# Logits of two batches as row sums on VectorE instead of transposes and matmuls on TensorE

## Chip, core and metric

One core of a Trainium2 chip runs the whole program. The metric is the time of one execution in microseconds (us) as the device counts it. Of the kernel before there are three timed runs and one profiled run.

## What is computed

Three layers follow one another: a causal attention with a decay, an up and down projection with a squared ReLU, and a layer of eight experts in which every expert takes 288 of the 2304 tokens, chosen by the size of their gate logits. In the change only the logits matter:

```python
x = attention(q, k, v, f)            # 2304 tokens of 512, in 4 batches of 576
h = np.maximum(x @ w_in, 0.0)        # 512 -> 2048
x2 = h * h @ w_out                   # 2048 -> 512
logits = x2 @ w_gate                 # 512 -> 8, float32
order = np.argsort(-logits.flatten())
# tokens are given to experts in this order, 288 to each
out[mask] = np.maximum(x2[mask] @ w1[e], 0.0) @ w2[e]     # for every expert e
```

## The kernel before

Every operation is entered as a task with the engines that may do it, an estimated cost on each, the buffers it reads and writes and a priority (`s.base`, then the order of entry; a lower number goes first). `Sched.run` (line 169) plays the whole program through once with these costs, gives each free engine the ready task of the lowest number, and so fixes for each engine the order of its instructions. On the chip each engine works in that order and waits for what is not ready.

The middle layer works in chunks of 256 tokens, `moe1_chunk(b, c)` (line 725), for batch b and half c, in the order (0,1), (0,0), (1,1), (1,0), (2,1), (2,0), (3,1). A chunk has 16 steps f. In a step `moe1_up` (line 683) makes 128 of the 2048 columns: 12 matmuls of 256 columns (lines 691 to 693: high by high, low by high, high by low part), then ScalarE takes the ReLU (696) and the square (697), a rounded high part `hh` is made, and the rest `hl` = r - `hh` (line 708) on GpSimd or VectorE. Two steps later `moe1_down` (lines 715 to 717) adds this step's six matmuls of 512 columns to two accumulators `acc`, one for each 128 tokens.

At the end of a chunk `x2_tail` (line 802) runs once for each of the two accumulators: the accumulator is copied to SBUF (`x2_rows`, line 791), stored to `x2d` in HBM, transposed by TensorE in four blocks (line 809), copied to SBUF again (812), multiplied with the gate matrix `wg` (line 817: four matmuls with 8 columns, each in two passes), and copied into the table of logits `L` (819). The buffers for rows and transposed rows are the two raw-weight buffers `wraw`; the transposes and logits use the two PSUM buffers `u` of the up projection.

The last two chunks, (3,0) and the 64 first tokens of all batches, go through `moe1_last` (line 744). It gets its logits in another way: `gate_weights` (line 822) sums on VectorE the products of each row of `w_out` and each gate column (16 blocks x 8 experts, line 835), so that the logits follow from the squared hidden values by short matmuls (lines 757, 758). The gate's columns for that lie on all partitions in `wgb`, loaded by one DMA from `wgT`. These tasks have priority 12, the chunks 3 + 2b.

The pools of these late stages open at barriers in the plan: `pp` and `gp` when the attention's tasks are done, `hp` (the hidden values of `moe1_last`) when the tasks of `gp` are done.

The routing (`phase`, line 934) takes the logits of the first three batches as one part and the rest as another, and sets the gather of the first expert's rows (line 1167) and with it the experts' matmuls (lines 1254 to 1288).

Of the kernel before, what the change touches and what calls it, by code (L numbers as in the profile page):

```python
# [8 lines left out]
F = mybir.dt.float32  # L9
R = mybir.dt.float32r  # L10
BF = mybir.dt.bfloat16
# [3 lines left out]
OP = mybir.AluOpType  # L15
# [4 lines left out]
B, H, S, D = 4, 8, 576, 64  # L20
NT, DM, DFF, E, FE = 2304, 512, 2048, 8, 1024
# [15 lines left out]
P0 = None  # L37
HV = [0]
NSM = 4
ABASE = (0, 0.5, 0.6, 2)  # L40
HM = 50.0
LM = 40.0
# [278 lines left out]
def dve1(n):  # L321
    return 70 + 1.04 * n
# [6 lines left out]
def act(n, psum=False, extra=0):  # L329
    return (51 if psum else 93) + 0.833 * n + 93 * extra  # L330
# [19 lines left out]
LO_ENG = ["pool"]  # L350
# [3 lines left out]
def hi_alts(n, engs="act pool"):  # L354
    a = {}
    for e in engs.split():
        a[e] = {"act": act(n), "pool": pts(n), "dve": dve2(n)}[e]
    return a


def lo_alts(n, engs=None):
    a = {}
    engs = engs or LO_ENG[0]
    for e in engs.split():
        a[e] = {"pool": ptt(n), "dve": dve1(n)}[e]
    return a


class K:
# [355 lines left out]
    def moe1_chunk(self, b, c):  # L725
        s = self.s
        xh, xl = self.moe1_x(b, c)
        acc = [s.buf(self.ps, [128, 512], F, "acc", 2) for _ in range(2)]

        def down(f):  # L730
            for t in range(2):
                self.moe1_down(f, t, acc[t], *prev[f])
        prev = []
        for f in range(16):
            prev.append(self.moe1_up(f, xh, xl))
            if f >= 2:
                down(f - 2)
        down(14)
        down(15)
        for t in range(2):  # L740
            self.x2_tail(b, c, t, acc[t])


    def moe1_last(self, chunks):
# [40 lines left out]
                self.x2_rows(b, c, t, acc[t])  # L785
        self.x2_done = s.tasks[-3]

    def x2_rows(self, b, c, t, acc):
        s, mp = self.s, self.mp
        xr = s.buf(mp, [128, 512], F, "x2r", 0, also=[("wraw", 0), ("wraw", 1)])  # L790
        s.op({"act": act(512, True), "dve": dve1(512)}, lambda e: self.rnd(e, xr.t, acc.t), r=[acc], w=[xr])
        tt = (b * 4 + c * 2 if b < B else 16) + t
        if b < B:
            tok = b * S + 64 + c * 256 + t * 128
            self.dma(lambda: self.x2d[tok:tok + 128, :], lambda: xr.t, 128 * 2048, r=[xr], w=[(self.x2d, tt)])
        else:
            for j in range(2):
                tok = (2 * t + j) * S
                self.dma(lambda tok=tok: self.x2d[tok:tok + 64, :], lambda j=j: xr[64 * j:64 * j + 64], 64 * 2048, r=[xr], w=[(self.x2d, (tt, j))])
        return xr, tt  # L800
# [18 lines left out]
        s.op({"act": act(8, True), "dve": dve1(8)}, lambda e: self.rnd(e, self.L[:, tt, :], pl[:, :E]), r=[pl], w=[(self.L, tt)])  # L819


    def gate_weights(self):
        s = self.s
        gp = self.gp
        wb = s.buf(gp, [128, E, DM], F, "wgb")
        self.dma(lambda: wb.t.rearrange("p e d -> p (e d)"), lambda: self.wgT.t.rearrange("e d -> (e d)")[None, :].to_broadcast([128, DM * E]), 128 * 16384, r=[self.wgT], w=[wb])
        Gf = s.buf(gp, [128, 16, E], F, "gf")
        G2 = self.G2 = s.buf(self.pp, [128, 16, 2 * E], R, "g2")
        for f in range(16):
            wo = s.buf(gp, [128, DM], F, "wof", 2)  # L830
            wh, wl = self.wu[self.unit(1, f, 0)]
            s.op(lo_alts(DM, "dve"), lambda e, f=f, wo=wo, wh=wh, wl=wl: e.tensor_add(wo.t, wh[:, f % 2].bitcast(F), wl[:, f % 2].bitcast(F)), r=[(wh, f % 2), (wl, f % 2)], w=[wo])
            for x in range(E):
                jk = s.buf(gp, [128, DM], BF, "gjk", 1)
                s.op({"dve": dve1(DM) + 85}, lambda e, f=f, x=x, wo=wo, jk=jk: e.tensor_tensor_reduce(  # L835
                    out=jk.t, in0=wo.t, in1=wb[:, x, :], scale=1.0, scalar=0.0, op0=OP.mult, op1=OP.add,
                    accum_out=Gf[:, f, x:x + 1]), r=[wo, wb], w=[jk, (Gf, (f, x))])
        n = 16 * E
        s.op(hi_alts(n, "act"), lambda e: self.rnd(e, G2[:, :, 0:E], Gf.t), r=[Gf], w=[G2])
        s.op({"dve": dve1(n)}, lambda e: e.tensor_sub(G2[:, :, E:], Gf.t, G2[:, :, 0:E].bitcast(F)), r=[Gf], w=[G2])  # L840
# [72 lines left out]
    def route_iotas(self):  # L913
# [4 lines left out]
        def bank():  # L918
            if not rt:
                rt.append(self.ps.tile([128, 512], F, name="ov0", tag="ov0", bufs=1))  # L920
            return rt[0]
        s.views["rt", 0] = lambda: bank()[:, 0:128]
        for j in range(NSM):
            s.views["rt", 1 + j] = lambda j=j: bank()[:, 128 + 64 * j:192 + 64 * j]
# [9 lines left out]
    def phase(self, m):  # L934
# [11 lines left out]
        def small(tag="sm"):  # L946

            if m == 0 and tag in ("H", "pl"):
                return s.buf(self.ps, [128, 512], F, tag + "0", 0, also=[("pt", 0)] if tag == "H" else [("sc", 0), ("sc", 1)])
            return s.buf(self.ps, None, F, tag, 0, also=[("rt", 0)] if tag == "H" else [("rt", 1 + j) for j in range(NSM)])  # L950

# [361 lines left out]
@with_exitstack  # L1313
def tile_kernel(ctx, tc, qT, kT, vP, f, w_in, w_out, w_gate, w1, w2, out, upto=9, dbg=None):
    k = K(ctx, tc, qT, kT, vP, f, w_in, w_out, w_gate, w1, w2, out)
    nc = tc.nc
    LO_ENG[0] = "pool"
    k.scat = []
    k.main_es, k.att_es = ExitStack(), ExitStack()
    s = k.s  # L1320
    k.early_pools()
    k.moe1_weights()
    k.att_pools()
    s.base = 0
    k.consts()
    k.cum()
    s.base = 50
    k.route_consts()
    s.base = 0
    s.base = 0  # L1330
    for b in range(B):
        s.base = ABASE[b]
        k.attention(b)
    s.base = 1
    s.pools["wraw"] = k.mp
    for which, r, c in [(w, r, c) for i in range(4) for w, r, c in [(0, r, i) for r in range(4)] + [(1, 4 * i + r, 0) for r in range(4)]]:
        t = k.unit(which, r, c)
        raws, was = [z for z in RS if z[1] > 2 * t + 1], [z for z in WS if z[1] > 2 * t + 1]
        hold = k.mark[0, WHD] if 4 * t > NE else None
        for half in [None] if raws else [0, 1]:  # L1340
            k.w_piece(which, r, c, half, raws or [("wraw", j) for j in range(2)], was, hold)
    s.base = 2
    k.gate_rows()
    for b in range(B):
        if b == 1:
            LO_ENG[0] = "dve pool"
        s.base = 3 + 2 * b
        for c in (1, 0) if b + 1 < B else (1,):
            k.moe1_chunk(b, c)

    def open_pp():
        k.att_es.close()
        k.pp.p = k.pool("pp", reuse_waits="tile")
        k.gp.p = k.pool("gp", ctx=k.gp_es, reuse_waits="tile")

    def open_hp():
        k.gp_es.close()
        k.hp.p = k.pool("hp", ctx=k.hp_es, reuse_waits="tile")

    def open_ep():  # L1360
        k.hp_es.close()
        k.main_es.close()
        k.ep.p = k.pool("ep", reuse_waits="tile")

    k.pp, k.gp, k.hp, k.ep = Late(), Late(), Late(), Late()
    k.gp_es, k.hp_es = ExitStack(), ExitStack()
    k.pp.bar = k.gp.bar = s.barrier(s.tasks_on(k.ao), open_pp)
    s.base = 12
    k.gate_weights()
    k.hp.bar = s.barrier(s.tasks_on(k.gp), open_hp)  # L1370
    s.base = 11
    k.moe1_last([(B - 1, 0), (B, 0)])
    k.ep.bar = s.barrier(s.tasks_on(k.xp, k.mp, k.hp), open_ep)
    LO_ENG[0] = "dve pool"
    s.base = 15
    k.route_iotas()
    for m in range(E):
        s.base = 20 + m
        idx, widx = k.phase(m)
        s.base = 30 + m  # L1380
        k.expert(m, idx, widx)
    order = s.run()
    s.emit(order)
# [34 lines left out]
```

## Time and profile before

| | us |
|---|---|
| median of three timed runs | 1013.84 |
| lowest and highest | 1009.37 and 1014.49 |
| profiled execution | 1011.21 |
| its span, first to last instruction | 1009.4 |

The profile is of one execution. A matmul that is listed as 0.28 us long overlaps with the next one, so what a piece of TensorE work takes out of the stream is read from the distance between starts. Idle time of an engine that nothing waits for costs nothing. PEclk is the granted TensorE clock: 1.00 is 2.4 GHz and 0.50 is 1.2 GHz.

### The profile page before, as it was taken

Reading aid. Unit: us, or ns where it says so; the run is one execution under the profiler, and the core shown is the slowest. Engines: PE = TensorE matmul, PEld = TensorE weight load, DVE = VectorE, ACT = ScalarE, POOL = GpSimd, SP = SyncE. Lnnn points to the kernel's source line nnn. Section 1 sums busy time; section 2 is a strip of 40 time slices with the busy share of each in tenths; the row PEclk is TensorE's granted clock in tenths of the full one; section 3 lists DMA queues with packets and bytes.
Section 4 is the critical chain, followed back from the end, with each engine's and each line's share of the span. In section 5 each row is a group of like instructions: output and inputs, shape, how many; then the busy total and the mean of one; then the engine's idle time right before and its main releaser. Section 6 shows DMA issues by size and latency. Waiting matters only on the chain. (4 is left out here: it accounts for less than half of the span.)

```text
span 1009.4 us, 17558 instructions
## 1 busy us (share of the span) xinstructions
PE 942.6 (93%) x6231; PEld 761.1 (75%) x6231; DVE 600.1 (59%) x1941; ACT 393.8 (39%) x1072; POOL 321.3 (32%) x439
## 2 busy tenths in 40 slices
PE   6897899899999999999999999995999989999996
PEld 3454555667789888989898899874777767778996
DVE  6899898974439999822223222476667786422231
ACT  4575676565534444434343356300101120224320
POOL 2555555652333333300010100001112041556921
PEclk9898899999999999999999999997899998999998
DMA  6668676542230101010100000015745541334410
GB/s 215 218 207 274 209 244 220 177 146 85 82 130 1 43 1 42 2 43 1 42 1 22 1 22 1 1 43 149 250 173 192 190 152 43 103 114 150 131 48 24
DMA packets 48616, 105.67 MB, mean 105 GB/s; under 512 B 10280, under 2 KB 18632, under 8 KB 48400
## 3 DMA queue, kind: packets, MB, share of 16 engines
q1 hardware_dynamic: 45456, 95.11, 28.5%
q0 software_dynamic: 3072, 9.44, 3.2%
q8 instruction: 49, 0.80, 0.3%
q14 instruction: 39, 0.32, 0.1%
HBM read 90.20 MB, written 14.33 MB: 104 GB/s over the span
## 5 line engine op out<-in xcount | busy, mean ns | idle before, releaser
L691 PE MATMUL u<-xh,z 128*128 128x256 f32 x512 | 148.9, 291 | 2.3 <-ACT r L696 1.9
L692 PE MATMUL u<-xh,z 128*128 128x256 f32 x512 | 145.6, 284 | 0.0
L693 PE MATMUL u<-xl,z 128*128 128x256 f32 x512 | 145.4, 284 | 0.0
L696 ACT ACTIVATE r<-u 128x256 f32<-128x256 f32 x144 | 54.7, 380 | 175.8 <-PE u L693 167.3
L835 DVE CUSTOM_DVE_ANT_0 gjk<-wof,wgb 128x512 bf16<-128x512 f32 x128 | 106.7, 833 | 11.6 <-ACT r L696 7.9
L691 PEld LDWEIGHTS u<-xh,z 128*128 128x128 f32 x512 | 98.1, 192 | 15.4 <-issue 3.1
L692 PEld LDWEIGHTS u<-xh,z 128*128 128x128 f32 x512 | 98.3, 192 | 8.1
L693 PEld LDWEIGHTS u<-xl,z 128*128 128x128 f32 x512 | 98.2, 192 | 0.0
L1283 PE MATMUL acc<-ehh,z 128*128 128x288 f32 x320 | 92.1, 421 | 0.0
L717 PE MATMUL acc<-z,hl 128*128 128x512 f32 x224 | 89.2, 398 | 1.9 <-POOL hl L708 1.6
L715 PE MATMUL acc<-z,hh 128*128 128x512 f32 x224 | 90.9, 406 | 0.0
L716 PE MATMUL acc<-z,hh 128*128 128x512 f32 x224 | 89.7, 400 | 0.0
L1254 PE MATMUL u<-exh,z 128*128 128x288 f32 x304 | 86.5, 420 | 0.1
L708 POOL TENSOR_TENSOR hl<-r,hh 128x256 fp32r<-128x256 f32 x64 | 56.0, 877 | 93.7 <-ACT hh L383 71.7
L708 DVE TENSOR_TENSOR hl<-r,hh 128x256 fp32r<-128x256 f32 x48 | 21.5, 447 | 92.9 <-ACT hh L383 79.9
L1206 POOL TENSOR_TENSOR z<-wr,z 128x512 fp32r<-128x512 f32 x48 | 61.1, 1305 | 48.0 <-ACT z L383 47.9
L523 ACT ACTIVATE p<-p,st 128x448 f32<-128x448 f32 (+4 forms) x109 | 59.9, 550 | 38.0 <-DVE st L516 36.2
L1283 PEld LDWEIGHTS acc<-ehh,z 128*128 128x128 f32 x320 | 57.5, 194 | 15.9 <-issue 1.6
L511 POOL TENSOR_TENSOR row<-maskb,row 128x128 f32<-128x128 bf16 (+1 forms) x90 | 46.5, 523 | 67.4 <-DVE st L516 39.3
L1254 PEld LDWEIGHTS u<-exh,z 128*128 128x128 f32 x304 | 55.5, 194 | 14.6 <-DVE exh L387 0.3
L697 ACT ACTIVATE r<-r 128x256 f32<-128x256 f32 x138 | 57.6, 418 | 4.1
L1167 POOL DMA_INDIRECT xg<-x2d,ph_idx x24 | 25.6, 1069 | 98.6 <-DVE ph_P L1109 51.9
(350 smaller groups left out, 2175.8 us busy)
## 6 DMA issues: line engine op xcount, KB each, us to landing
z<-in_w_dram SPq DMA_DIRECT2D x36, 512.0 KB
wr<-in_w_dram SPq DMA_DIRECT2D x24, 512.0 KB
z<-in_w_in_dram SPq DMA_DIRECT2D x16, 512.0 KB
z<-in_w_out_dram SPq DMA_DIRECT2D x14, 512.0 KB
row<-cumd SPq DMA_DIRECT2D x24, 288.0 KB
xd<-xo SPq DMA_DIRECT2D x16, 288.0 KB
wraw<-rd SPq DMA_DIRECT2D x32, 128.0 KB
xa<-xd SPq DMA_DIRECT2D x8, 512.0 KB
```

Source lines behind the costliest of these rows:

```text
L523: s.op({"act": act(w, extra=2)}, lambda e, x=x, si=si, i=i, n=n, w=w, p=p[x], st=st[x]: e.activation(p[:n, :w], p[:n, :w], AF.Exp, bias=st ...
L691: e.matmul(u[:, :256], wh[:, k % 2, fs], xh[k][1](), start=(k == 0), stop=False)
L692: e.matmul(u[:, :256], wl[:, k % 2, fs], xh[k][1](), start=False, stop=False)
L693: e.matmul(u[:, :256], wh[:, k % 2, fs], xl[k][1](), start=False, stop=(k == 3))
L708: s.op(lo_alts(256), lambda e: e.tensor_sub(hl(), r.t, hh().bitcast(F)), r=[r, kh], w=[kl])
L715: g = [lambda e: e.matmul(acc.t, hh()[:, ts], wh[:, f % 2], start=(f == 0), stop=False), lambda e: e.matmul(acc.t, hh()[:, ts], wl[:, f % ...
L716: lambda e: e.matmul(acc.t, hh()[:, ts], wl[:, f % 2], start=False, stop=False),
L717: lambda e: e.matmul(acc.t, hl()[:, ts], wh[:, f % 2], start=False, stop=(f == 15))]
L835: s.op({"dve": dve1(DM) + 85}, lambda e, f=f, x=x, wo=wo, jk=jk: e.tensor_tensor_reduce(out=jk.t, in0=wo.t, in1=wb[:, x, :], scale=1.0, sc ...
L1206: s.op(lo_alts(512, LOE(m, which, i, 0, c)), lambda e, cs=cs: e.tensor_sub(lo[:, cs], raw[:, cs], hi[:, cs].bitcast(F)), r=[(raw, key), (h ...
L1254: s.op({"pe": 1.69 * CAP}, lambda e, k=k: e.matmul(u[:, :CAP], whi[0][k][:, fs], xh[k].t, start=(k == 0), stop=(k == 3)), r=[(whi[0][k], c ...
L1283: e.matmul(acc[:, :CAP], wh[:, ds], hh.t, start=(f == 0), stop=(f == 7))
```

## The change

The chunks of batches 1 and 2 (four chunks, eight accumulators) call a new function `x2_sums` instead of `x2_tail`. It copies the accumulator to a buffer `x2g` that takes the place of one of the attention's two `xo` buffers, stores it to `x2d` as before, and then issues eight VectorE instructions. Each multiplies the 128 x 512 rows with one gate column that lies on all partitions and adds along the row into one column of `L`. The transposes, the copy of the transposed rows, the logit matmuls and the copy of the logits of these chunks are gone. Each sum has a planned cost of 887 ns on VectorE.

For that the load of `wgb` is taken out of `gate_weights` into `gate_load`, and it and the barrier that opens `pp` and `gp` are entered ahead of the chunks. The load has priority 2 instead of 12. The barrier of `hp` now also waits in the plan for the eight times eight sums, since they use `gp`.

```diff
+DL = (1, 2)
...
         for t in range(2):
-            self.x2_tail(b, c, t, acc[t])
+            (self.x2_sums if b in DL else self.x2_tail)(b, c, t, acc[t])
...
+    def x2_sums(self, b, c, t, acc):
+        s = self.s
+        xr = s.buf(self.xp, [128, DM], F, "x2g", 0, also=[("xo", 0), ("xo", 1)])
+        xr.after = self.gp.bar
+        xr, tt = self.x2_rows(b, c, t, acc, xr)
+        for x in range(E):
+            jk = s.buf(self.gp, [128, DM], BF, "gjs", 1)
+            s.op({"dve": dve1(DM) + 285}, lambda e, x=x, jk=jk: e.tensor_tensor_reduce(
+                out=jk.t, in0=xr.t, in1=self.wgb[:, x, :], scale=1.0, scalar=0.0, op0=OP.mult, op1=OP.add,
+                accum_out=self.L[:, tt, x:x + 1]), r=[xr, self.wgb], w=[jk, (self.L, tt)])
...
-    def x2_rows(self, b, c, t, acc):
+    def x2_rows(self, b, c, t, acc, xr=None):
         s, mp = self.s, self.mp
-        xr = s.buf(mp, [128, 512], F, "x2r", 0, also=[("wraw", 0), ("wraw", 1)])
+        xr = xr or s.buf(mp, [128, 512], F, "x2r", 0, also=[("wraw", 0), ("wraw", 1)])
...
+    def gate_load(self):
+        s = self.s
+        wb = self.wgb = s.buf(self.gp, [128, E, DM], F, "wgb")
+        self.dma(lambda: wb.t.rearrange("p e d -> p (e d)"), lambda: self.wgT.t.rearrange("e d -> (e d)")[None, :].to_broadcast([128, DM * E]), 128 * 16384, r=[self.wgT], w=[wb])
+
     def gate_weights(self):
         s = self.s
         gp = self.gp
-        wb = s.buf(gp, [128, E, DM], F, "wgb")
-        self.dma(lambda: wb.t.rearrange("p e d -> p (e d)"), lambda: self.wgT.t.rearrange("e d -> (e d)")[None, :].to_broadcast([128, DM * E]), 128 * 16384, r=[self.wgT], w=[wb])
+        wb = self.wgb
...
     k.gate_rows()
+    k.pp, k.gp, k.hp, k.ep = Late(), Late(), Late(), Late()
+    k.gp_es, k.hp_es = ExitStack(), ExitStack()
+    k.pp.bar = k.gp.bar = s.barrier(s.tasks_on(k.ao), open_pp)
+    k.gate_load()
     for b in range(B):
...
             k.moe1_chunk(b, c)
...
-    k.pp, k.gp, k.hp, k.ep = Late(), Late(), Late(), Late()
-    k.gp_es, k.hp_es = ExitStack(), ExitStack()
-    k.pp.bar = k.gp.bar = s.barrier(s.tasks_on(k.ao), open_pp)
     s.base = 12
     k.gate_weights()
```

## Rows read from the trace of the kernel before

**Rows 1.** The profile's page, part 1: busy time, share of the span, instructions of each engine.

```profile
PE 942.6 (93%) x6231; PEld 761.1 (75%) x6231; DVE 600.1 (59%) x1941; ACT 393.8 (39%) x1072; POOL 321.3 (32%) x439
```

**Rows 2.** Busy time by stage: two chunks of the middle stretch; the columns stand first.

```profile
core 0: us, PE busy (x) PEld busy (x) DVE busy (x) ACT busy (x) POOL busy (x), PEclk, DMA share, GB/s
...
340.00:390.00 50.00, 48.96 (x315) 43.74 (x314) 48.06 (x113) 22.29 (x55) 17.77 (x19) 1.00 0.07 22
...
440.00:490.00 50.00, 49.96 (x326) 45.29 (x326) 10.51 (x23) 19.50 (x49) 4.18 (x7) 1.00 0.08 22
```

**Rows 3.** TensorE in order of time, end of chunk (1,1): start, length, work, count, wait.

```profile
384.50 0.60 PE L809 MATMUL u<-ident,wraw 128*128 128x128 f32 x4
385.36 0.66 PE L809 MATMUL u<-ident,wraw 128*128 128x128 f32 x4 [0.26 <-ACT r L696]
385.78 0.48 PE L715 MATMUL acc<-z,hh 128*128 128x512 f32 x1
...
387.24 1.84 PE L817 MATMUL u<-wg,wraw 128*128 128x8 f32 x16
388.94 0.37 PE L691 MATMUL u<-xh,z 128*128 128x256 f32 x1
```

**Rows 4.** The same view, end of chunk (1,0).

```profile
433.07 1.29 PE L809 MATMUL u<-ident,wraw 128*128 128x128 f32 x8
434.12 0.48 PE L715 MATMUL acc<-z,hh 128*128 128x512 f32 x1
...
435.09 1.85 PE L817 MATMUL u<-wg,wraw 128*128 128x8 f32 x16
436.79 0.41 PE L691 MATMUL u<-xh,z 128*128 128x256 f32 x1
```

**Rows 5.** The same view, end of chunk (2,0).

```profile
531.30 1.09 PE L809 MATMUL u<-ident,wraw 128*128 128x128 f32 x8
532.32 0.50 PE L715 MATMUL acc<-z,hh 128*128 128x512 f32 x1
...
534.02 1.95 PE L817 MATMUL u<-wg,wraw 128*128 128x8 f32 x16 [0.38 <-DVE wraw L387]
535.83 0.45 PE L691 MATMUL u<-xh,z 128*128 128x256 f32 x1
```

**Rows 6.** Busy time, columns as in Rows 2, behind the second and the fourth chunk end.

```profile
436.98:440.25 3.27, 3.27 (x14) 2.98 (x14) 0.16 (x1) 0.00 (x0) 0.00 (x0) 0.50 0.00 0
...
536.00:539.30 3.30, 3.30 (x14) 3.01 (x14) 3.22 (x17) 0.00 (x0) 0.00 (x0) 0.50 0.00 0
```

**Rows 7.** VectorE's existing row sums, line 835: ns min/median/max, starts; then the page's mean.

```profile
L835 DVE CUSTOM_DVE_ANT_0 gjk<-wof,wgb x128: 676/693/1257, 300.3 to 422.3; 128x512 bf16<-128x512 f32 x128
L835 DVE DVE_READ_ACCUMULATOR2_ANT gf<- x128: 75/81/85, 300.9 to 422.9; 128x1 f32 x128
L835 DVE CUSTOM_DVE_ANT_0 gjk<-wof,wgb 128x512 bf16<-128x512 f32 x128 | 106.7, 833 | 11.6 <-ACT r L696 7.9
```

**Rows 8.** Low halves hl from 300 to 423 us: engine, durations; who waited for them.

```profile
L708 POOL TENSOR_TENSOR hl<-r,hh x37: 728/891/1287, 301.2 to 421.0; 128x256 fp32r<-128x256 f32 x37
...
  PE acc L717: 1.6, 3
```

**Rows 9.** The same view from 440 to 580 us.

```profile
L708 DVE TENSOR_TENSOR hl<-r,hh x43: 424/426/953, 442.9 to 578.5; 128x256 fp32r<-128x256 f32 x43
```

**Rows 10.** All engines in order of time: TensorE's longest wait for a low half.

```profile
382.02 0.50 PE L717 MATMUL acc<-z,hl 128*128 128x512 f32 x1 [0.67 <-POOL hl L708]
```

**Rows 11.** The SP queue in order of time: the load of the gate's columns.

```profile
292.97 0.34 SPq L390 DMA_DIRECT2D wgb<-wgT  x1
```

**Rows 12.** First use of the gate weights' product, line 757: starts at the end.

```profile
L757 PE MATMUL sc<-h,g x8: 280/280/291, 583.2 to 602.0; 128*16 128x256 f32 x8
```

**Rows 13.** VectorE in order of time, where the routing starts.

```profile
645.87 0.39 DVE L387 COPY L<-u 128x8 f32<-128x8 f32 x2 [0.83 <-PE u L775]
```

**Rows 14.** TensorE's waits from 640 to 725 us: total, times, longest.

```profile
PE pt L1234 <- DMA xg<-x2d,ph_idx: 6.1, 1, 6.1
```

More of the change, by code (lines that the diff above doesn't have):

```diff
@@ L1343, in tile_kernel @@
     k.gate_rows()
[L1344 to L1349, printed above, removed]
     def open_pp():
@@ L1367, in tile_kernel @@
     k.pp.bar = k.gp.bar = s.barrier(s.tasks_on(k.ao), open_pp)
+    k.gate_load()
+    for b in range(B):
+        if b == 1:
+            LO_ENG[0] = "dve pool"
+        s.base = 3 + 2 * b
+        for c in (1, 0) if b + 1 < B else (1,):
+            k.moe1_chunk(b, c)
     s.base = 12
```

## The prediction

> **What bounds the kernel now.** I read the page's shares first: TensorE is busy for 93% of the span, VectorE for 59%, and no other engine comes near [rows 1]. A share is an average, so the busy time by stage comes next. In the stretch of the chunks, from 290 to 590 us, TensorE is busy for 48.96 us of 50 in one stage and 49.96 in another, at the full clock; VectorE is full in the first (48.06 of 50) and nearly idle in the second, 10.51 of 50 [rows 2]. What fills it in the first are the row sums for the gate weights, 128 of them between 300.3 and 422.3 us [rows 7]. Then I read TensorE in order of time at the ends of the four chunks that the change touches, where the reader is to see two pieces that interrupt the stream of 256- and 512-column matmuls: the transposes (line 809) and the logits (line 817) [rows 3 to 5]. So the bound of this stretch is TensorE, and the question is what its stream loses and whether VectorE's new work makes it wait.
>
> **What TensorE is rid of.** Listed lengths overlap, so I take the distance from the start of a piece to the start of the next other matmul. Chunk (1,1): 384.50 to 385.78 is 1.28 us for eight transposes, of which 0.26 is a wait for a free `u` buffer, and 387.24 to 388.94 is 1.70 for 16 logit matmuls; together 2.98 [rows 3]. Chunk (1,0): 433.07 to 434.12 is 1.05 and 435.09 to 436.79 is 1.70, together 2.75 [rows 4]. Chunk (2,1) repeats these two lengths at 482.8 and 484.8: 2.75. Chunk (2,0): 531.30 to 532.32 is 1.02, 534.02 to 535.83 is 1.81, and ahead of the logits stands a wait of 0.38 for the copy of the transposed rows; together 3.21 [rows 5]. The sum is 2.98 + 2.75 + 2.75 + 3.21 = 11.7 us, all of it on the engine that sets the pace.
>
> **What the clock gives back.** Right behind the logits of the second and of the fourth of these chunks the granted clock is 0.50 (1.2 GHz) for 3.27 and 3.30 us, with the engine's stream unbroken [rows 6]; elsewhere in the stages shown it is 1.00 [rows 2]. What the engine did just before was 16 matmuls of 8 columns each. At half the clock it does half the work, so these cost (3.27 + 3.30) / 2 = 3.3 us. But behind the first and the third of them, with the same pieces, there is no such fall, so that they end with the logits is an inference. I count them as gained and put the case in which they stay among the rivals; the bounds of this term are 0 and 3.3.
>
> **What VectorE gets.** 64 sums of the form that is already there: two 512-element float32 operands in SBUF, a bfloat16 product thrown away, one accumulator read. One takes 833 ns in the mean (676 to 1257) and its read 81 [rows 7]; at 0.833 + 0.081 = 0.914 us a chunk end gets 16 x 0.914 = 14.6 us, and all four 58.5 us. In a stage of 50 us like the second one VectorE has 39 us free [rows 2], so three of the blocks fit whole. The first, at some 387 us, falls among the gate weights. The sums have the lower number (5 against 12), so the gate weights end some 15 us later, near 438 instead of 423; their product is first used at 583.2 [rows 12], 145 us on. The barrier of `hp` now waits for the last block too; that ends near 550 in the time of the old trace and the hidden values of the last chunks are first needed around 580, so it costs nothing while that margin of some 30 us holds. The row buffers cost nothing: the attention's output buffers are empty before the load at 293 [rows 11], and the first chunk end that wants one is at 384 [rows 3].
>
> **What that makes late.** While VectorE is full the low halves go to GpSimd: 37 of them there between 300 and 423 us, 891 ns in the median, against 426 ns on VectorE when that is free [rows 8, 9]. From the logits of one chunk to those of the next, 387.24 to 435.09, are 47.9 us and 16 steps [rows 3, 4], so a step takes 3.0; a low half is wanted two steps later, so 0.5 us more on its way is mostly covered. TensorE lost 1.6 us to late low halves in these 123 us [rows 8], the longest single wait being 0.67 [rows 10]. At that rate 58.5 us of a full VectorE cost 1.6 / 123 x 58.5 = 0.8 us, which I take. The bounds are 0, if every low half is covered, and four times the longest wait, 2.7; a gain from this I exclude, since nothing on VectorE gets faster by it.
>
> **What is moved.** The load of the gate's columns stands on SP's queue at 292.97, behind the attention's last store [rows 11]. It cannot start earlier, because its pool opens when the attention is done, and nothing of the chunks stands right behind it, so priority 2 instead of 12 changes nothing. Without that cover it would delay one chunk's load by the time of its own 2 MB: VectorE's first sum on it starts at 300.3 [rows 7], so by at most 7.3 us, once. The copies that fall away (two of 512 and two of 8 elements in each chunk end, on ScalarE or VectorE) lie on engines that have room, and their gain is in the waits counted above. With one store of rows per accumulator before and after, the DMA queue carries the same.
>
> **Does the gain reach the end?** The routing starts when the last logits are copied at 645.87, right behind TensorE [rows 13]; the gap of TensorE behind it ends with the gather of the first expert's rows, a wait of 6.1 us [rows 14], and that gather waits for the routing and for rows that TensorE has just made. Nothing in this chain is tied to an earlier event, so it should move as a whole.
>
> **The sum.** 11.7 + 3.3 - 0.8 = 14.2 us. From the profiled execution's 1011.2 that gives 997.0. That execution lies 2.6 us below the median of the three runs (1013.84), which by itself would make 999.6; I go halfway, 998.
>
> **A rule against it.** The Trainium skill, page "SBUF — State Buffer", section "SBUF: two separate sides", says that VectorE and GpSimd share a pair of ports that one of them holds for a whole instruction, a VectorE instruction with two SBUF inputs among them. The trace agrees as far as it goes: the same sum takes between 676 and 1257 ns, the same low half on GpSimd between 728 and 1287 [rows 7, 8]. If GpSimd were shut out for a whole block rather than for one instruction, the change would be a loss, and that is the third rival.
>
> **The rivals.** First, the clock: the half-speed stretches come all the same, there or elsewhere. Then the gain is 11.7 - 0.8 = 10.9, and the time some 1001.5. For it speaks that two of four ends had none while doing the same. Chance 0.2.
>
> Second, the change takes away what it says but TensorE idles in its place: the transposes and logits filled the time in which a new chunk waits for its first low halves. Then the 11.7 us come back as waits and only the clock's 3.3 stay, some 1009. Against it: behind each of these pieces matmuls follow without a gap [rows 3, 4], so there was ready work. Chance 0.1.
>
> Third, slower: the low halves of the next chunk's first steps come behind the whole block of 16 sums, in VectorE's order or at the shared ports. The sums have the lower number, so VectorE takes them first. A block of 14.6 us less the two steps of 6.0 that are covered is 8.6 us of idle TensorE per chunk end, 34 in all; less the 15.0 of the gains that is 19 slower, some 1032. It decides from the point where low halves wait for more than six sums in a row. Against it speaks that among 128 such sums 37 low halves went through GpSimd and none took over 1287 ns [rows 8]. Chance 0.08.
>
> **How the numbers follow.** Forecast 0.62, by its bounds 993 to 1003 with the spread of the runs; clock rival 0.2; idle rival 0.1; slower rival 0.08. Half a per cent, 5 us, is about what a measurement of this kernel can tell from no change, so faster means under 1008.8: the first two cases whole and a little under half of the third, 0.85; within: the rest of the third and a slower rival cut short, 0.08; slower 0.07. The range for 8 in 10 runs from 991 to 1008.
>
> **What would show it.** Right: TensorE busy without the two pieces at the four chunk ends, a clock of 1.00 through the stretch from 340 to 540, low halves on GpSimd for some 15 us behind each of the four, and the last logits at about 632 instead of 646. Wrong: waits of TensorE at line 717 for low halves of several us in all, a stretch at 0.50 behind a chunk end that has no logits any more, or last logits that come early and a gather that does not.

## Result

| | us |
|---|---|
| before, median of 6 timed runs | 1012.17 (1008.24 to 1014.92) |
| changed, median of 6 timed runs | 998.52 (993.28 to 1000.60) |
| ratio, 95% interval | 0.9861 (0.9826 to 0.9895) |
| profiled execution, before and changed | 1011.21 and 997.44 |
| its span, before and changed | 1009.4 and 995.7 |

The change is 1.4% faster. Part 1 of the changed kernel's page, the line that answers to [rows 1], in the same columns:

```profile
PE 929.3 (93%) x6135; PEld 749.8 (75%) x6135; DVE 637.0 (64%) x2037; ACT 392.1 (39%) x1068; POOL 344.9 (35%) x459
```

TensorE has lost 96 instructions and 13.3 us of busy time, VectorE has 37 us more, GpSimd 24 us more. TensorE's share is the same 93%: it still sets the pace.

Where the time went is read best between fixed points of the stream. I take the start of the copy of each chunk's first accumulator; the list below is every such copy in order of time, ScalarE's and VectorE's, of the kernel before, for the chunks (0,0), (1,1), (1,0), (2,1), (2,0), (3,1):

```profile
332.86 1.29 ACT L383 ACTIVATE wraw<-acc 128x512 f32<-128x512 f32 x2 [2.69 <-DVE gf L835]
382.56 1.31 ACT L383 ACTIVATE wraw<-acc 128x512 f32<-128x512 f32 x2 [2.70 <-PE acc L717]
430.79 1.38 DVE L387 COPY wraw<-acc 128x512 f32<-128x512 f32 x2 [1.22 <-PE acc L717]
480.52 1.38 DVE L387 COPY wraw<-acc 128x512 f32<-128x512 f32 x2 [1.22 <-PE acc L717]
529.10 1.38 DVE L387 COPY wraw<-acc 128x512 f32<-128x512 f32 x2 [1.42 <-PE acc L717]
580.04 1.38 DVE L387 COPY wraw<-acc 128x512 f32<-128x512 f32 x2 [0.59 <-PE acc L717]
```

VectorE's copies of logits of the kernel before (ns min/median/max, first and last start); the last start closes the stage:

```profile
L387 DVE COPY L<-u x13: 159/167/168, 390.4 to 646.1; 128x8 f32<-128x8 f32 x13
```

The same two of the changed kernel, where the middle four go to the `xo` buffers:

```profile
333.54 1.29 ACT L385 ACTIVATE wraw<-acc 128x512 f32<-128x512 f32 x2 [2.70 <-PE acc L719]
383.20 1.31 ACT L385 ACTIVATE xo<-acc 128x512 f32<-128x512 f32 x2 [2.70 <-PE acc L719]
429.27 1.31 ACT L385 ACTIVATE xo<-acc 128x512 f32<-128x512 f32 x2 [1.86 <-PE acc L719]
474.79 1.38 DVE L389 COPY xo<-acc 128x512 f32<-128x512 f32 x2 [1.23 <-PE acc L719]
520.28 1.38 DVE L389 COPY xo<-acc 128x512 f32<-128x512 f32 x2 [1.42 <-PE acc L719]
565.86 1.39 DVE L389 COPY wraw<-acc 128x512 f32<-128x512 f32 x2 [0.59 <-PE acc L719]
```

Its copies of logits on VectorE, in the columns of the list above:

```profile
L389 DVE COPY L<-u x6: 165/166/167, 571.3 to 631.9; 128x8 f32<-128x8 f32 x6
```

The distances, in us (each holds the end of the chunk named first in its row):

| from, to | before | changed | less by | forecast for it |
|---|---|---|---|---|
| (0,0) to (1,1) | 49.70 | 49.66 | 0.04 | 0 |
| (1,1) to (1,0) | 48.23 | 46.07 | 2.16 | 2.98 - 0.8 = 2.2 |
| (1,0) to (2,1) | 49.73 | 45.52 | 4.21 | 2.75 + 1.63 = 4.4 |
| (2,1) to (2,0) | 48.58 | 45.49 | 3.09 | 2.75 |
| (2,0) to (3,1) | 50.94 | 45.58 | 5.36 | 3.21 + 1.65 = 4.9 |
| (3,1) to the last logits | 66.06 | 66.04 | 0.02 | 0 |
| the whole stage | 313.24 | 298.36 | 14.88 | 14.2 |

(The 0.8 of waits stands in the row in which it turned up.) The half us that the row of (2,0) has over its forecast is two pauses at that end of the kernel before:

```profile
530.90 0.28 PE L693 MATMUL u<-xl,z 128*128 128x256 f32 x1
...
533.14 0.50 PE L717 MATMUL acc<-z,hl 128*128 128x512 f32 x1
```

The transposes start 0.40 us behind the first of these lines and the logits 0.88 behind the second [rows 5]; elsewhere in the chunks such matmuls are followed after 0.12 and 0.23. That is 0.28 + 0.65 us of pause, of which the forecast has 0.38. Outside the stage the changed execution reached the first mark 0.68 us later and took 363.8 instead of 363.3 us from the last logits to the end; 0.68 - 14.88 + 0.5 = -13.7 is the difference of the spans.

The end of chunk (1,0) in the changed kernel, TensorE in order of time, which answers to [rows 4]:

```profile
426.15 0.50 PE L719 MATMUL acc<-z,hl 128*128 128x512 f32 x1 [0.54 <-POOL hl L710]
...
428.73 0.50 PE L719 MATMUL acc<-z,hl 128*128 128x512 f32 x1 [0.53 <-DVE hl L710]
429.07 0.40 PE L717 MATMUL acc<-z,hh 128*128 128x512 f32 x1
429.31 0.40 PE L718 MATMUL acc<-z,hh 128*128 128x512 f32 x1
429.55 0.40 PE L719 MATMUL acc<-z,hl 128*128 128x512 f32 x1
429.78 0.28 PE L693 MATMUL u<-xh,z 128*128 128x256 f32 x1
```

The last matmul of the accumulator is followed 0.23 us later by the next chunk's, and no transposes come. The two waits of 0.54 and 0.53 are the price. TensorE's busy time and clock behind this end and behind (2,0)'s, in stretches of 5 us with the columns of [rows 2], against the 0.50 of [rows 6]:

```profile
430.00:435.00 5.00, 5.00 (x39) 4.79 (x38) 4.96 (x15) 3.82 (x9) 1.84 (x2) 1.00 0.46 168
435.00:440.00 5.00, 5.00 (x32) 4.43 (x31) 5.00 (x15) 1.22 (x3) 2.32 (x3) 1.00 0.00 0
520.00:525.00 5.00, 4.88 (x38) 4.51 (x37) 4.31 (x9) 1.57 (x4) 1.61 (x2) 1.00 0.28 105
525.00:530.00 5.00, 5.00 (x29) 4.30 (x28) 4.79 (x13) 1.60 (x4) 3.10 (x4) 1.00 0.01 3
```

VectorE's new sums, the old ones, and the low halves from 300 to 600 us (ns min/median/max, starts); the second list answers to [rows 7], the third to [rows 8, 9]:

```profile
L798 DVE CUSTOM_DVE_ANT_0 gjs<-xo,wgb x64: 677/692/1228, 385.3 to 535.5; 128x512 bf16<-128x512 f32 x64
```

```profile
L853 DVE CUSTOM_DVE_ANT_0 gjk<-wof,wgb x128: 675/692/1226, 301.2 to 441.0; 128x512 bf16<-128x512 f32 x128
```

```profile
L710 POOL TENSOR_TENSOR hl<-r,hh x59: 732/1043/1276, 299.4 to 541.2; 128x256 fp32r<-128x256 f32 x59
L710 DVE TENSOR_TENSOR hl<-r,hh x33: 412/425/954, 354.8 to 564.3; 128x256 fp32r<-128x256 f32 x33
```

The new sums cost what the old ones do, 692 ns in the median. The old ones end at 441 us instead of 422, so they now reach over the end of chunk (1,0).

### The profile page after: what moved, and what is told of

It reads as the page before. It is cut to its first block, busy times and chain, and to the rows that moved or that the text cites. A ratio compares the mean times of both kernels' runs of the same rounds, so it can differ in the third digit from the quotient of the medians.

```text
span 995.7 us, 17474 instructions
## 1 busy us (share of the span) xinstructions
PE 929.3 (93%) x6135; PEld 749.8 (75%) x6135; DVE 637.0 (64%) x2037; ACT 392.1 (39%) x1068; POOL 344.9 (35%) x459
## 5 line engine op out<-in xcount | busy, mean ns | idle before, releaser
L710 POOL TENSOR_TENSOR hl<-r,hh 128x256 fp32r<-128x256 f32 x79 | 74.7, 947 | 117.4 <-ACT hh L385 100.7
L1324 POOL DMA_INDIRECT out_dram<-yo,ph_idx x24 | 24.3, 1011 | 100.8 <-DVE ph_q L1034 32.7
```

The lines of the kernel that those rows point to most:

```text
L710: s.op(lo_alts(256), lambda e: e.tensor_sub(hl(), r.t, hh().bitcast(F)), r=[r, kh], w=[kl])
```

## Experiments

All times are ratios to runs of the kernel before on the same chip, with the 95% interval; such a ratio is not the quotient of two medians. The whole time scatters by several us between executions of one program, mostly outside the stage, so beside the ratio I give the stage: from the first copy of (0,0)'s accumulator to the last logits in the profiled execution (313.2 before, 298.4 changed).

| kernel | median us | ratio (95%) | stage us |
|---|---|---|---|
| e1: load and barrier early, no sums | 1011.05 | 1.0011 (0.9977 to 1.0044) | 311.7 |
| e2: second batch only | 1009.49 | 0.9991 (0.9963 to 1.0019) | 308.4 |
| e3: sums over 64 elements | 997.03 | 0.9876 (0.9822 to 0.9930) | 299.8 |
| e4: every sum twice | 1000.39 | 0.9903 (0.9868 to 0.9939) | 299.7 |
| e5: transposes kept | 1004.92 | 0.9914 (0.9881 to 0.9947) | 303.4 |
| e6: logit matmuls kept | 1007.72 | 0.9959 (0.9925 to 0.9994) | 305.4 |
| e13: the same program, one execution | 1003.49 | none | 307.0 |
| e12: both kept | 1008.76 | 0.9971 (0.9946 to 0.9997) | 309.6 |
| e7: also (0,0) | 997.27 | 0.9862 (0.9820 to 0.9905) | 295.0 |
| e8: also (3,1) | 995.38 | 0.9832 (0.9792 to 0.9872) | 301.8 |
| e11: also (0,0) and (3,1) | 992.85 | 0.9825 (0.9794 to 0.9857) | 298.0 |
| e14: the change again | 994.45 | 0.9853 (0.9816 to 0.9891) | 298.5 |

**e1, the order alone.**

```diff
-DL = (1, 2)
+DL = ()
```

> The load of the gate's columns and the barrier are entered early as in the change, but no chunk uses the sums. My theory (the gain is TensorE's 11.7 us of transposes and logits, 3.3 us of clock, less some 1 us of waits): no difference from the kernel before, within 2 us, with both half-speed stretches behind chunk ends still there. Rival (the other order of load and barriers brings part of it): 4 us or more below the kernel before.

No difference, so the earlier load and barrier bring nothing. The clock fell behind one chunk end, (2,0), and not behind two, which makes the stage 1.5 us shorter: that the falls come in the same places each time was wrong.

**e2, one batch.**

```diff
-DL = (1, 2)
+DL = (1,)
```

> The sums for the second batch only (chunks (1,1) and (1,0)). My theory: 2.98 + 2.75 us of TensorE work and 1.6 us of clock behind (1,0), less some 1 us where the gate weights, pushed back by the first block of sums, meet the end of (1,0): 6.3 us below the kernel before, ratio 0.994, and a clock of 0.50 behind (2,0) as before. Rival (the half-speed stretches come anyway): 4.7 us below, ratio 0.995, with a half-speed stretch behind (1,0) or a new one elsewhere.

Missed: the ratio says 1 us below the kernel before and the medians 2, not 6.3, and the interval leaves room for 3.7 at most. The stage was 4.8 us shorter, and the distances of the changed part are those of the full change: 46.08 and 45.50 between the marks (46.07 and 45.52 there). What eats the rest in the profile is the clock behind (2,0), whose logits are still there:

```profile
530.00:535.00 5.00, 5.00 (x26) 4.71 (x26) 3.26 (x18) 0.00 (x0) 0.00 (x0) 0.60 0.02 3
535.00:540.00 5.00, 5.00 (x27) 4.74 (x27) 1.19 (x3) 2.19 (x6) 0.00 (x0) 0.72 0.00 0
```

(0.40 + 0.28) x 5 = 3.4 us lost, twice as much as in the kernel before behind one end. Without it the stage would be 305.0, 4.95 below the kernel before without its two falls (313.24 - 3.29 = 309.95); the two ends are worth 5.73 less the 0.8 of waits. So the parts of the sum hold in the stage; whether the long fall is usual in this kernel one profile can't say. The timed runs point that way: their mean granted clock is 0.9688, against 0.9709 in the 28 runs of the kernel before beside them, and 0.0021 of 1008 us is 2.1 us less of full clock. That would account for the better part of what the whole time lacks; why it is so is open.

**e3, shorter sums.**

```diff
-            s.op({"dve": dve1(DM) + 285}, lambda e, x=x, jk=jk: e.tensor_tensor_reduce(
-                out=jk.t, in0=xr.t, in1=self.wgb[:, x, :], scale=1.0, scalar=0.0, op0=OP.mult, op1=OP.add,
+            s.op({"dve": dve1(64) + 285}, lambda e, x=x, jk=jk: e.tensor_tensor_reduce(
+                out=jk[:, :64], in0=xr[:, :64], in1=self.wgb[:, x, :64], scale=1.0, scalar=0.0, op0=OP.mult, op1=OP.add,
```

The planned cost of a sum is shortened with it, so the order of the instructions changes too.

> As the changed kernel, but each sum runs over the first 64 of the 512 elements, so that the logits of these two batches are other numbers and tokens go to other experts, 288 to each as before. My theory: VectorE's blocks shrink to about a third, the gate weights no longer reach into the end of (1,0), and the waits of TensorE for low halves go back from 2.6 to some 1.6 us: about 1 us below the changed kernel. Rival (the blocks of sums hold TensorE up in ways that the waits don't show, by order or ports): 3 us or more below the changed kernel.

The ratio can't be told from the changed kernel's. The stage holds a fall of the clock behind (3,1), whose logits are still done by matmuls; without its 1.7 us it is 298.1, against 298.4. The three distances from (1,1) to (2,0) are 47.04, 45.06 and 44.90, together 137.0, against 137.1 in the change. Nothing is won by a VectorE that has less to do, so the 1 us that I expected was too much, and the rival's 3 us is not there in the stage. The reason for the 1 us did not come either: the gate weights' sums still start up to 430.9 us, just ahead of the mark of (1,0) at 432.5, and TensorE's waits for low halves are 2.3 us, not 1.6.

**e4, sums twice.**

```diff
-        for x in range(E):
+        for x in [y for y in range(E) for _ in range(2)]:
```

> As the changed kernel, but every sum is issued twice, so each block on VectorE is 29 us instead of 14.6. My theory: low halves go to GpSimd for twice as long and are covered all the same; 1 to 3 us above the changed kernel, still some 10 us below the kernel before. Rival (low halves wait behind the whole block): each block holds TensorE up by 14.6 us more, over 30 us above the changed kernel, slower than before.

The sums, now 128 (ns min/median/max, starts), and below them TensorE's waits for GpSimd's low halves from 300 to 580 us (total, times, longest):

```profile
L798 DVE CUSTOM_DVE_ANT_0 gjs<-xo,wgb x128: 677/692/1232, 389.0 to 560.2; 128x512 bf16<-128x512 f32 x128
```

```profile
PE acc L719 <- POOL hl L710: 3.6, 7, 0.7
```

Twice the work on VectorE costs 1.3 us of stage; the waits go from 2.6 us in all to 3.6, none over 0.7. A block of 29 us does not hold the low halves up. So the slower rival falls.

**e5 and e6, one piece back at a time.** The four chunk ends get back the transposes (with the copy) or the logit matmuls (with the copy), whose results nothing uses.

```diff
         xr, tt = self.x2_rows(b, c, t, acc, xr)
+        s.op({"pe": 530.0}, tr, r=[xr], w=[pt])
...
+        s.op({"act": act(512, True), "dve": dve1(512)}, lambda e: self.rnd(e, xt.t, pt.t), r=[pt], w=[xt])
```

```diff
         xr, tt = self.x2_rows(b, c, t, acc, xr)
+                e.matmul(pl[:, :E], xr[:, k * 128:(k + 1) * 128], self.wg[:, k, :], start=(k == 0), stop=(k == 3))
...
+        s.op({"pe": 896.0}, lg, r=[xr, self.wg], w=[pl])
+        lx = s.buf(self.gp, [128, E], F, "lx", 2)
+        s.op({"act": act(8, True), "dve": dve1(8)}, lambda e: self.rnd(e, lx.t, pl[:, :E]), r=[pl], w=[lx])
```

The first diff is e5, the second e6; the functions that are entered are those of `x2_tail`.

> As the changed kernel, but the four touched chunks also keep the transposes of their rows and the copy of the transposed rows, whose results nothing uses; the logit matmuls stay out. Stage from the first copy of (0,0)'s accumulator to the last logits: 313.2 us before, 298.4 changed. My theory (the transposes are worth 4.2 us, the logits the rest, and the half-speed stretches come only behind logits): 302.6 in the stage, some 1003 in all, clock 1.00 behind the four chunk ends. Rival (the half-speed stretches come from the transposes or from the whole end of a chunk): one or more stretches at 0.50 behind the four chunk ends, 304 or more.

> As the changed kernel, but the four touched chunks also keep the logit matmuls of 8 columns, on the rows as they are and not transposed, and copy their results to a buffer that nothing uses; the transposes stay out. My theory: 298.4 + 6.9 = 305.3 us in the stage for the matmuls alone, and a clock of 0.50 behind some of the four chunk ends, 1.6 us for each stretch: 305 to 309, some 1006 to 1010 in all. Rival (the stretches have nothing to do with the logits): 305.3 with a clock of 1.00 behind all four.

e5: stage 303.4, 5.0 above the change (4.2 expected), clock 1.00 behind all four ends. TensorE's waits for low halves are 3.1 us there instead of 2.6, the longest 1.3, and it waits another 1.1 for `u` buffers. e6: stage 305.4, 7.0 above the change (6.9 expected), and again a clock of 1.00 behind all four. So the size of the logits is right, that of the transposes short by the waits that come with them, and where the falls come from was open. A second execution of the program of e6:

> A second look at the kernel that keeps the logit matmuls and no transposes, for the clock alone. If logits without transposes are enough for a fall of the clock behind a chunk end, about four ends in ten would show one, as in the profiles with both pieces (4 of 10), so one to two of these four; if it takes both pieces and the waits between them, none, as in the first look.

The stretch behind the end of (2,0), first in e6:

```profile
525.00:530.00 5.00, 4.88 (x37) 4.42 (x35) 3.20 (x8) 1.60 (x6) 0.64 (x1) 1.00 0.30 108
530.00:535.00 5.00, 5.00 (x35) 4.61 (x35) 4.79 (x12) 1.08 (x5) 0.96 (x2) 1.00 0.00 0
```

and in e13:

```profile
525.00:530.00 5.00, 4.88 (x34) 4.39 (x33) 4.52 (x12) 1.83 (x6) 1.60 (x2) 0.86 0.30 108
530.00:535.00 5.00, 5.00 (x28) 4.45 (x28) 3.34 (x10) 1.22 (x3) 0.46 (x1) 0.80 0.00 0
```

Here is a fall without any transposes, at the same place of the same program that had none before. It costs (0.14 + 0.20) x 5 = 1.7 us, and the stages differ by 307.0 - 305.4 = 1.6.

**e12, both pieces back.** The tasks of e5 and after them those of e6, with the matmuls on the transposed rows:

```diff
+        s.op({"pe": 530.0}, tr, r=[xr], w=[pt])
...
+        s.op({"pe": 896.0}, lg, r=[xt, self.wg], w=[pl])
```

> As the changed kernel, but the four touched chunks keep the transposes and the logit matmuls as well, whose results go to a buffer that nothing uses: the sums are added and nothing is taken away. My theory (all of the gain is TensorE's work and its clock, VectorE's sums cost about 1 us): 298.4 + 11.7 + 1 = 311 us in the stage without a fall of the clock, up to 315 with two of them as in the kernel before; the time within 3 us of the kernel before. Rival (the sums themselves cost more, hidden in the gain so far): 4 us or more above the kernel before.

The first mark, the last logits, and TensorE at the end of (2,0):

```profile
332.81 1.31 ACT L385 ACTIVATE wraw<-acc 128x512 f32<-128x512 f32 x2 [2.69 <-PE acc L719]
L389 DVE COPY L<-u x6: 166/167/168, 583.7 to 642.4; 128x8 f32<-128x8 f32 x6
```

```profile
533.24 0.96 PE L808 MATMUL u<-wg,wraw 128*128 128x8 f32 x8
534.05 0.36 PE L693 MATMUL u<-xh,z 128*128 128x256 f32 x1
...
535.18 0.95 PE L808 MATMUL u<-wg,wraw 128*128 128x8 f32 x8
535.99 0.37 PE L693 MATMUL u<-xh,z 128*128 128x256 f32 x1
```

Stage 309.6 with no fall of the clock, 11.2 above the change. The kernel before without its two falls has 309.95. So with all of TensorE's work back the sums on VectorE add nothing that can be seen in the stage, and the pieces are worth 11.2 us. But the order is not that of the kernel before: the logits come as eight and eight matmuls with others between them, not as 16 in a row. For the clock these four ends are therefore another case, and the ratio of 0.9971, below 1 in line with the missing falls, does not say why they are missing.

**e7, one chunk more.**

```diff
-            (self.x2_sums if b in DL else self.x2_tail)(b, c, t, acc[t])
+            (self.x2_sums if b in DL or (b, c) == (0, 0) else self.x2_tail)(b, c, t, acc[t])
```

> As the changed kernel, and chunk (0,0) too takes the sums. My theory: its end is worth another 1.28 + 1.70 us of TensorE, and the gate weights, pushed back by one more block of 14.6 us, still end some 115 us before their use: stage 295.5 us, 2 to 3 us below the changed kernel. Rival (VectorE's backlog now lies over two chunk ends and costs there): as the changed kernel or slower.

Stage 295.0, 3.4 below the change, a little more than expected: the (0,0) to (1,1) distance is 46.29 instead of 49.66, the others are as in the change. Its ratio is equal to the change's within the interval; 3 us in 1000 is less than these runs resolve.

**e8 and e11, the chunk ahead of the barrier.**

```diff
-DL = (1, 2)
+DL = (1, 2, 3)
```

> As the changed kernel, and chunk (3,1) too takes the sums, so that the barrier of the hidden values' pool waits in the plan for its sums. My theory of the change says that this margin was what kept the barrier free of cost; here it is gone: the chunk's sums end some 15 us behind its last matmul while the hidden values of the last chunks are wanted at once. 2.9 us of TensorE saved and 5 to 12 us of waits: slower than the changed kernel by 2 us or more. Rival (the barrier costs nothing at all, since those values also fit in freed weight buffers): 2 to 3 us below the changed kernel.

The wait came as expected. In the kernel with (3,1), TensorE's wait at the first hidden values of the last chunks, ScalarE's rounding of them (each line with the wait ahead of it), and the busy time in stretches of 5 us:

```profile
575.34 0.40 PE L760 MATMUL sc<-h,g 128*16 128x256 f32 x1 [7.88 <-POOL h L710]
```

```profile
574.50 0.42 ACT L385 ACTIVATE h<-r 128x256 fp32r<-128x256 f32 x1 [8.82 <-DVE L L798]
```

```profile
565.00:570.00 5.00, 2.45 (x21) 2.15 (x19) 4.79 (x14) 0.65 (x2) 0.00 (x0) 1.00 0.02 7
570.00:575.00 5.00, 0.00 (x0) 0.00 (x0) 4.26 (x15) 0.42 (x1) 0.45 (x1) 0.61 0.00 0
575.00:580.00 5.00, 4.67 (x22) 4.48 (x23) 1.77 (x3) 1.56 (x4) 1.43 (x3) 0.50 0.00 0
```

ScalarE may not write into the hidden values' pool until the last sum (line 798) has read the gate's columns that lay there. TensorE stands for 7.9 us, and the clock falls to 0.50 in it. The stage is 3.4 us longer than the change's, as expected. Yet the whole time is not longer, against the expectation: the experts' stage, from its first matmul to the end, took 290.9 us instead of 300.2, with another order of its instructions. To see whether that goes with the barrier, e11 takes both edits, that of e7 and that of e8, beside the change itself once more (e14):

> The sums for chunk (0,0), both halves of the second and third batch, and chunk (3,1). From the runs so far: (0,0) brings 3.4 us in the stage; (3,1) makes TensorE wait 7.9 us for the barrier, but with it the experts' stage had another order and was 9 us shorter. If that shorter order comes with the barrier's place: 3 us below the kernel with (3,1) alone, some 992. Rival (the order of the experts' stage falls out by chance of the plan): the experts' stage is back at 296 to 302 us and the time at 1000 or above.

> The changed kernel once more, beside the others of this call on one chip: ratio 0.986 to the kernel before, stage 298.4 us, clock 1.00 behind the four touched chunk ends.

e14 came as expected: ratio 0.9853, stage 298.5, clock 1.00 behind the four ends. e11 has the same wait of 7.9 us and again a short experts' stage, 289.7. But from the last logits to the first expert matmul e8 and e11 take 67.3 and 68.2 us, the two profiles of the change 63.6 and 62.6. From the last logits to the end it is 358.2 and 357.9 against 363.8 and 356.7: all within what two executions of the changed kernel differ by. So part of it is work put ahead instead of behind (376 instructions of TensorE between the last logits and the first expert matmul, against 340 in the change), and the rest is not told from scatter. e11 has the lowest median of all, 992.85, 1.6 us below the change beside it (e14); the intervals of the two overlap widely.

## Why the prediction was right

**What bounds the stretch** was right: removing TensorE's pieces shortened every touched distance and no untouched one (0.04 and 0.02).

**What TensorE is rid of**, 11.7 us, was right: putting both pieces back costs 11.2 (e12), the logits alone 7.0 (e6), the transposes alone 5.0 (e5). e5 and e6 sum to 12.0, so the distances between starts, read off the trace, were good to half a us in the sum. Piece by piece they were less good: they leave out the pauses ahead of a piece, as at the end of (2,0), and the waits that come with it (e5).

**What the clock gives back**, 3.3 us, came as counted in the profiled execution, but the step was luckier than its reasoning. Across the profiles the four touched ends had logit matmuls in 22 cases and a fall of the clock behind 5 of them (2 of 4 before, 1 of 4 in e1, 1 of 2 in e2, 1 of 4 in e13, none of 4 in e6 and e12), and no logit matmuls in 34 cases with no fall at all (the change twice, e2's other two, e3, e4, e5, e7, e8 and e11). So at these ends the falls go with the logits, and transposes are not needed for one; but they come in only a quarter of the cases, and one lasted twice as long. The place counts too: four of the five are behind (2,0), where four of six ends with logits had one and none of eight without. Behind (0,0) and (3,1), where 12 profiles each have logits, there is one fall in 24 (e3). What makes a fall come is not shown.

What one fall costs was right: from (1,0) to (2,1) are 49.73 us in the kernel before, with a fall, and 48.22 in e1, without. But as a mean the term is worth less than 3.3 us: the four ends of the kernel before and of e1 lost (3.3 + 1.7) / 2 = 2.5. The timed runs, which list their mean granted clock, say less still: (1 - clock) x span is 29.7 us in the mean of 65 runs of the kernel before and 28.5 in that of 12 runs of the change, 1.2 less with a standard error of 0.9 (an estimate, since a low clock under an idle engine counts in it too). Then some 13 us of the timed gain are not the clock's, where the sum had 11.7 - 0.8 = 10.9 and the stage shows 14.88 - 3.3 = 11.6; where the rest lies is not shown. That the sum of 14.2 hits the timed runs as well as it does is partly luck.

**What that makes late**, 0.8 us, was right in size: TensorE's waits for low halves from 300 to 580 us went from 1.6 to 2.6 us. The gate weights ended near the forecast, at 441 us for 438. The place was not where the prediction looked. It spoke of low halves behind the blocks of sums; two of the changed kernel's waits lie at the end of (1,0) instead, where the gate weights, moved back by the first block, meet the next chunk's first preparations. Behind the blocks themselves, of which the last three lie over an otherwise free VectorE, there was none from 430 to 580 us, and none over 0.7 us even when they were twice as long (e4).

**The barrier's margin** was the right thing to name: with one chunk more the margin is gone and TensorE waits 7.9 us (e8).

**That the gain reaches the end** was right for this change: 363.3 us from the last logits to the end before, 363.8 changed. A second execution of the change took 356.7 (e14), so that the two agree to half a us is chance.

**The rivals.** Idle in place of the work: no, the next matmul follows after 0.23 us, and behind (1,0) and (2,0) TensorE is busy for 19.88 of 20 us. Slower by low halves behind the block: no (e4). The clock: its premise, that an end with both pieces can go without a fall, holds (6 of the 10 in the kernel before, e1 and e2); its conclusion, that the falls come all the same, does not.

**The shared ports.** In the changed kernel a new sum takes between 677 and 1228 ns and a low half on GpSimd between 732 and 1276. Of the 192 sums between 300 and 600 us, old and new, the 79 with no GpSimd instruction beside them take at most 695 ns, the other 113 up to 1228. That agrees with the rule of the Trainium skill (page "SBUF — State Buffer", section "SBUF: two separate sides") that the two engines share ports which one of them holds for a whole instruction; that the ports are the reason no run here shows. GpSimd is not shut out for a whole block: with blocks of 32 sums no low half there takes over 1286 ns (e4).

## What to carry to other kernels

Where one engine is without gaps, take the price of a piece of its work from start to start of its neighbours, and move the piece to an engine with idle time in that very stretch; a count of 39 us free in a stage of 50 is worth more than an average of 59%. What the move costs need not show beside the moved work: look at what the moved work pushes back, and at which barrier or buffer waits for its last reader. Check a gain of 1% in a stage of the trace between fixed marks, since the whole time of this kernel scatters by more than the effect of one chunk.

## What the runs showed of the hardware

The granted clock can fall to 0.50 for 3.4 us, once for 6.8 (e2), at the end of 16 float32 matmuls of 8 columns, with little idle time of TensorE: it is busy for 9.96 us of 10 around the fall behind (1,0) in the kernel before and for 9.41 of 10 around that behind (2,0). The same program shows a fall in one execution and not in the next (e6, e13).

A sum over 64 instead of 512 elements takes 224 instead of 692 ns in the median, so an eighth of the elements costs a third of the time: on a straight line through the two, (692 - 224) / 448 = 1.04 ns per element and 157 ns besides.

The same program took 300.2 and 294.1 us for the experts' stage in two executions of the changed kernel, with a mean granted clock of 0.97 and 0.98; a hundredth of some 297 us is 3 us, about half of the difference.
